# Windowed attention and SoLU feed-forward: the first tile's product block by block, w_in's differences on VectorE, scores moved on TensorE

## The chip, the cores and the metric

The kernel runs on one core of one Trainium2 chip. The metric is the time of one execution on the device in microseconds (us), as the median of several runs. A core has TensorE (PE in the rows; PEld are its weight loads), VectorE (DVE), ScalarE (ACT), GpSimd (POOL) and SyncE (SP), which here issues every DMA. Each engine takes its instructions in order; engines wait for each other by semaphores.

## The reference

Attention over a window of 64 keys, 8 batches of 576 positions with 8 heads of 64, and behind it a feed-forward layer with softmax gating and a normalization:

```python
scores = scale * np.matmul(q, k.transpose(0, 1, 3, 2))
scores = np.where((rel >= 0) & (rel < 64), scores, -1000000000.0)
attn = np.exp(scores - np.max(scores, axis=-1, keepdims=True))
attn = attn / (np.sum(attn, axis=-1, keepdims=True) + 1e-09)
x = np.matmul(attn, v)                  # heads joined: 4608 x 512
h = x @ w_in                            # 512 x 1024
e = np.exp(h - np.max(h, axis=-1, keepdims=True))
solu = h * (e / (np.sum(e, axis=-1, keepdims=True) + 1e-09))
ln = (solu - mu) / np.sqrt(var + 1e-06) * g_ln      # mean and variance of a row
return ln @ w_out                       # 1024 x 512
```

## The kernel before

The 4608 rows are 36 tiles of 128. A tile passes these steps, which are functions in the code (t is the tile):

- `scores(t)` (L376): 32 small matmuls of q and k into pS, of which there is one buffer. For a tile in `MASKED` (tiles 1 to 5) two more matmuls (L384) put the mask into pS first.
- `softmax(t)` (L407): for a tile in `MASKED`, VectorE takes the maximum out of pS by two reductions (L421), and eight exponentials on ScalarE (L437) read pS. For later tiles one VectorE instruction (L428) moves pS with scale and mask to sS, another (L433) takes the maximum, and the exponentials read sS. The scaling by the inverse sum, eight instructions (L452), is VectorE's for tiles below `SCALES` = 3 and GpSimd's from there.
- `transposes(t)` (L495), for tiles below 8: eight transposes on TensorE, copied in two halves to PT (L511); the second half by VectorE from tile `EARLY` = 3, else by ScalarE. From tile 8 the probabilities are turned by DMA instead (`soft_planes`, `soft_turn`: pd<-raw, raw<-pd).
- `values(t)` (L523): 32 matmuls with v into pX; ScalarE copies pX to xH (L538, L540), VectorE makes the rest xL (L541, from tile 3).
- `moe_in(t, h)` (L552): half h of the product with w_in into pH (one buffer). Tiles below `PLAIN_IN` = 3 use the plain float32 weights W32 in four matmuls a half (L556; two instructions each in the trace); later tiles use three passes with weights and x in two parts (L567).
- `moe_norm(t)` (L572): maximum (L582), exponential (L584), product and sum (L587), square (L593) and some small steps, then the scaling of e on GpSimd (L604).
- `moe_transpose(t)`, or by DMA `planes` and `turn`; then `moe_out(t)` (L679) with w_out: L685 for tile 0, L695 from tile 1, and the output copy ot (L702).

The weights come as int64 words of doubles, in eight blocks: 0 to 3 are w_in, 4 to 7 w_out. `weight_block` (L287) converts each by one ScalarE and four VectorE steps (L308 to L315); w_out is also multiplied by g on GpSimd (L319). `split(i)` (L330) makes the two parts of a block: ScalarE rounds each half to WH (L333), and the difference WL of half 0 is made by VectorE and that of half 1 by GpSimd (L336). The tiles WL lie in the same ring of nine buffers as W32: WL of block i + 1 overwrites W32 of block i, and so waits for all that reads that block, the differences of block i among it.

The order is made by a planner when the program is built. TensorE keeps the order in which the code lists the steps (but for the transposes, values and scores of tiles 0 and 1). The other engines' steps, SyncE's DMAs among them, get due times from it, counted back through the listed costs, and are placed by a list schedule. Where the schedule has TensorE idle, matmuls on the identity are put in (pO_filler, L784), until the first output product.

The loop from L736 lists, for each t below `BEHIND` = 3: both halves of `moe_in(t)`, `moe_norm(t)`, `planes(t)`, `transposes(t + 1)`, scores and softmax of tile t + 3, `values(t + 1)`. For t = 0 scores and softmax of tile 2 stand between the halves. From t = 3: `moe_in(t, 0)`, `transposes(t + 1)`, `moe_in(t, 1)`, `moe_norm(t)`, `planes(t)`, `moe_transpose(t - 3)`, `values(t + 1)`, the scores of the tiles in `ahead(t)`, `moe_out(t - 3)`. `ahead` gives tile 6 at t = 3, tiles 7 and 8 at t = 4, and t + 4 from there on. `split` of w_in is listed at t = 3, that of w_out at t = 4.

Of the kernel before, what the change touches and what calls it, by code (L numbers as in the profile page):

```python
# [24 lines left out]
NEG = -1.0e9  # L25

AHEAD = 3
FURTHER = 4

HASTE = 1  # L30
# [1 line left out]
LOOSE = 2  # L32
BEHIND = 3

EARLY = 3

JOINS = 8

PLANES = 4

HEADS = 1
MASKED = range(1, 6)
SCALES = 3

PLAIN_IN = 3
PLAIN_OUT = 1

BY_DMA = (1, 2)
# [137 lines left out]
def tile_window_attention_solu_moe(  # L186
# [17 lines left out]
    nc = tc.nc  # L204
# [125 lines left out]
    def split(i):  # L330

        for x in range(2):
            plan.op("ACT", 600, lambda x=x: nc.scalar.copy(WH(i, x), W32(i)[:, x]),  # L333
                    [("w", i), ("w", i, x), ("w", NC + 1 if i < NC else NW - 1)], [("H", i, x)])
            engine, eng, cost = (("DVE", nc.vector, 690), ("POOL", nc.gpsimd, 1450))[x]
            plan.op(engine, cost, lambda x=x, eng=eng: eng.tensor_sub(  # L336
                WL(i)[:, x], W32(i)[:, x], WH(i, x).bitcast(F32)),
                [("w", i), ("w", i, x), ("H", i, x)], [("w", NW + i, x)])
# [213 lines left out]
    def moe_in(t, h):  # L552
        hs = slice(h * 512, (h + 1) * 512)
        if t < PLAIN_IN:
            for c in range(NC):
                plan.op("PE", 930, lambda c=c: nc.tensor.matmul(  # L556
                    PH(t)[:, hs], XH(t)[:, c], W32(c)[:, h],
                    start=(c == 0), stop=(c == NC - 1)),
                    [("xH", t), ("w", c), ("w", c, h)], [("pH", t)])
            return  # L560
        passes = [(c, *k) for c in range(NC) for k in (
            (XH, WH, "xH", "H", 0), (XH, WL, "xH", "w", NW), (XL, WH, "xL", "H", 0))]
        if t == PLAIN_IN:

            passes.sort(key=lambda k: k[4] == "w")
        for n, (c, x, w, xk, wk, o) in enumerate(passes):
            plan.op("PE", 233, lambda n=n, c=c, x=x, w=w: nc.tensor.matmul(  # L567
                PH(t)[:, hs], x(t)[:, c], WH(c, h) if w is WH else WL(c)[:, h],
                start=(n == 0), stop=(n == len(passes) - 1)),
                [(xk, t), (wk, o + c, h)], [("pH", t)])  # L570
# [108 lines left out]
    def moe_out(t):  # L679
# [22 lines left out]
        plan.op("ACT", 580, lambda: nc.scalar.copy(ot(), PO()), [("pO", t)], [("ot", t)])  # L702
        plan.dma(P * DM * 4, lambda: nc.sync.dma_start(out[t * P:(t + 1) * P, :], ot()), [("ot", t)], [])

    def on(f, t, *args):
        if 0 <= t < NTILE:
            f(t, *args)
# [28 lines left out]
    for t in range(NTILE + BEHIND):  # L736
# [4 lines left out]
            for i in range(NC):  # L741
                split(i)
        on(moe_in, t, 0)
        if t == 0:
            scores(2)
            softmax(2)
        if t < BEHIND:
            on(moe_in, t, 1)
            on(moe_norm, t)
            on(planes, t)  # L750
            on(transposes, t + 1)
            on(scores, t + AHEAD)
            on(softmax, t + AHEAD)
            on(soft_planes, t + AHEAD)
            on(soft_turn, t + AHEAD)
            on(join, t + 1)
            on(values, t + 1)
        else:
            on(transposes, t + 1)
            on(moe_in, t, 1)  # L760
            on(moe_norm, t)
            on(planes, t)
            if t - BEHIND < NTILE - BY_DMA[1]:
                on(moe_transpose, t - BEHIND)
            on(join, t + 1)
            on(values, t + 1)
            for a in ahead(t):
                on(scores, a)
                on(softmax, a)
                on(soft_planes, a)  # L770
                on(soft_turn, a)
            if t - BEHIND == PLAIN_OUT:
                for i in range(NC, NC + NF // 2):
                    split(i)
            if t - BEHIND + 1 >= NTILE - BY_DMA[1]:
                on(moe_transpose, t - BEHIND + 1)
            on(moe_out, t - BEHIND)

    plan.first = [("qk", 0), ("raw", 0), ("v", 0), ("qk", 1), ("raw", 1), ("raw", 2), ("raw", 3), ("v", 1), ("qk", 2)]
    def filler(n):  # L780
# [53 lines left out]
```

## Time and profile before

| | |
|---|---|
| median of 3 runs | 548.37 us (546.87 to 548.4) |
| profiled execution | 549.3 us; its span, first to last instruction, 547.5 us |
| TensorE (PE) busy | 530.9 us, 97% of the span |
| VectorE (DVE) | 367.4 us, 67% |
| ScalarE (ACT) | 330.3 us, 60% |
| GpSimd (POOL) | 292.9 us, 53% |
| chain that ended last | PE 84%, DVE 7%, POOL 3%, DMA 2% |

The page gives busy time per engine over the whole span, which is an average over unlike stages: the start, in which the weights are converted and the first tiles pass, the steady part, and the end. The rows further down are from views of the same execution that look at one stage, one engine or one line. TensorE's busy time includes the filling matmuls, and matmuls overlap, so a matmul's cost in a row of them is the distance from start to start. A releaser behind an idle time is the instruction that the waiting one waited for last. The granted clock is TensorE's, 1.00 for 2.4 GHz and 0.50 for 1.2 GHz.

### The profile page before, as it was taken

To read this page: it belongs to the slowest core of one execution; us is meant where nothing else is said; L and a number is where in the kernel's file an instruction comes from. 1 tells how busy PE (TensorE), PEld (TensorE's weight loads), DVE (VectorE), ACT (ScalarE), POOL (GpSimd) and SP (SyncE) were. 2 spreads that over 40 slices of the span, in tenths; PEclk is the share of its full clock that TensorE was granted. 3 is DMA by queue.
4 is the path that set the end of the run, shared out by engine and by line. 5 is a ranking of instruction groups with operands and counts; after the bars stand their busy time and mean duration, and the time that the engine had idled before them with its cause. 6 is when DMAs were issued, how large, how long until landed. Compare 5 with 4: busy or idle time off the path is not lost.

```text
span 547.5 us, 11649 instructions
## 1 busy us (share of the span) xinstructions
PE 530.9 (97%) x4250; PEld 416.9 (76%) x4250; DVE 367.4 (67%) x725; ACT 330.3 (60%) x955; POOL 292.9 (53%) x490
## 2 busy tenths in 40 slices
PE   8799799899999999999999999999999999999996
PEld 7565486688877877778778777777877777777885
DVE  4999758766666666666666666666666677655530
ACT  4468475576666666666666666656666666663330
POOL 5214988664555555555555555555555555671110
PEclk9999989899999999999999999999999999999999
DMA  8963115647999999999999999999999994787211
GB/s 355 403 262 116 48 59 168 209 146 208 236 255 233 242 246 237 257 234 242 241 256 231 246 261 217 243 262 222 262 243 237 246 233 155 189 235 174 59 38 38
DMA packets 153081, 115.58 MB, mean 211 GB/s; under 512 B 129856, under 2 KB 129856, under 8 KB 152512
## 3 DMA queue, kind: packets, MB, share of 16 engines
q1 hardware_dynamic: 153024, 114.84, 81.0%
q8 instruction: 33, 0.54, 0.4%
q14 instruction: 24, 0.20, 0.1%
HBM read 41.42 MB, written 41.42 MB: 151 GB/s over the span
## 4 chain that ended last, share of the span: by engine, by line
PE 84%; DVE 7%; POOL 3%; issue 2%; DMA 2%; ACT 1%; SPq 0%; POOLq 0%; ACTq 0%
PE pO L695 35%; PE pH L567 33%; PE pX L530 6%; PE pS L400 5%; DMA raw<-pd 2%; DVE w L313 1%; PE pO L685 1%; DVE w L315 1%; PE pH L556 1%; POOL e L604 1%; DVE w L309 1%; PE t L506 1%; DVE sS L452 1%; POOL w L336 1%; POOL sS L452 1%
## 5 line engine op out<-in xcount | busy, mean ns | idle before, releaser
L452 POOL TENSOR_SCALAR sS<-sS,rec 128x128 f32<-128x128 f32 x264 | 117.4, 467 | 147.1 <-DVE rec L449 144.7
L695 PE MATMUL pO<-w_outH,yH 128*128 128x512 f32 x280 | 115.3, 412 | 0.7 <-ACT ot L702 0.7
L695 PE MATMUL pO<-w,yH 128*128 128x512 f32 x280 | 111.6, 399 | 0.0
L695 PE MATMUL pO<-w_outH,yL 128*128 128x512 f32 x280 | 110.6, 395 | 0.0
L567 PE MATMUL pH<-w_inH,xH 128*128 128x512 f32 x264 | 106.5, 403 | 0.0
L567 PE MATMUL pH<-w,xH 128*128 128x512 f32 x264 | 104.2, 398 | 0.0
L567 PE MATMUL pH<-w_inH,xL 128*128 128x512 f32 x264 | 104.1, 394 | 0.0
L437 ACT ACTIVATE sS<-sS,nmx 128x128 f32<-128x128 f32 x248 | 96.2, 390 | 9.6 <-DVE nmx L433 4.7
L702 ACT COPY ot<-pO 128x512 f32<-128x512 f32 x36 | 21.1, 587 | 97.8 <-PE pO L695 77.4
L584 ACT ACTIVATE e<-pH,mst 128x1024 f32<-128x1024 f32 x36 | 40.2, 1118 | 59.1 <-DVE mst L582 58.8
L582 DVE TENSOR_REDUCE mst<-pH 128x1 f32<-128x1024 f32 x36 | 44.1, 1224 | 42.0 <-PE pH L567 42.0
L604 POOL TENSOR_SCALAR e<-e,mst 128x512 f32<-128x512 f32 x72 | 60.1, 843 | 16.8 <-DVE mst L601 14.9
L596 DVE SCALAR_TENSOR_TENSOR mst<-mst 128x1 f32<-128x1 f32 x36 | 27.8, 772 | 60.1 <-ACT pl L593 60.1
L695 PEld LDWEIGHTS pO<-w_outH,yH 128*128 128x128 f32 x280 | 52.9, 189 | 18.0 <-issue 4.8
L695 PEld LDWEIGHTS pO<-w_outH,yL 128*128 128x128 f32 x280 | 53.0, 189 | 13.2
L695 PEld LDWEIGHTS pO<-w,yH 128*128 128x128 f32 x280 | 52.9, 189 | 10.9
L567 PEld LDWEIGHTS pH<-w_inH,xH 128*128 128x128 f32 x264 | 49.9, 189 | 13.2 <-ACT sS L437 0.2
L567 PEld LDWEIGHTS pH<-w_inH,xL 128*128 128x128 f32 x264 | 50.1, 190 | 12.4
L567 PEld LDWEIGHTS pH<-w,xH 128*128 128x128 f32 x264 | 49.6, 188 | 11.4 <-issue 0.2
L472 POOL COPY raw<-sS 128x1024 uint16<-128x1024 uint16 x56 | 56.7, 1043 | 0.0
L437 ACT ACTIVATION_READ_ACCUMULATOR sS<-sS,nmx 128x1 f32 x248 | 46.6, 188 | 0.0
L663 DVE TENSOR_TENSOR yL<-yT,yH 128x512 fp32r<-128x512 f32 x66 | 44.5, 708 | 2.6 <-ACT yH L661 2.6
(95 smaller groups left out, 867.0 us busy)
## 6 DMA issues: line engine op xcount, KB each, us to landing
qk<-qk SPq DMA_DIRECT2D x36, 640.0 KB, 5.9
yd<-pl SPq DMA_DIRECT2D x33, 512.0 KB, 6.6
pd<-raw SPq DMA_DIRECT2D x28, 512.0 KB, 3.7
v<-vS SPq DMA_DIRECT2D x36, 256.0 KB, 3.4
y<-ot SPq DMA_DIRECT2D x36, 256.0 KB, 3.1
raw<-w_in SPq DMA_DIRECT2D x4, 1024.0 KB, 10.6
raw<-w_out SPq DMA_DIRECT2D x4, 1024.0 KB, 8.6
yT<-yd SPq DMA_TRANSPOSE x33, 4.8
```

The source lines that it names most:

```text
L400: nc.tensor.matmul(PS(t)[half * WIN:(half + 1) * WIN, r, p], q[rs, p, half * WIN:(half + 1) * WIN], keys, start=t not in MASKED, stop=t no ...
L437: plan.op("ACT", 580, lambda h=h: nc.scalar.activation(SS(t)[:, h], PS(t)[:, h // NPAIR, h % NPAIR] if t in MASKED else SS(t)[:, h], AF.Ex ...
L452: plan.op(engine, cost, lambda h=h: v.tensor_scalar(SS(t)[:, h], SS(t)[:, h], rec()[:, h:h + 1], 0.0, ALU.mult, ALU.add), [("rec", t)], [( ...
L472: plan.op(engine, cost, lambda x=x, copy=copy: copy(PP(t)[:, :, 4 * x:4 * x + 4].rearrange("p k h n -> p k (h n)"), SS(t)[:, 4 * x:4 * x + ...
L530: nc.tensor.matmul(PX(t)[r * D:(r + 1) * D, p, ks], (V if half else VX)(t)[:, h * D:(h + 1) * D], PT(t)[:, r * NPAIR + p, ks], start=True, ...
L567: plan.op("PE", 233, lambda n=n, c=c, x=x, w=w: nc.tensor.matmul(PH(t)[:, hs], x(t)[:, c], WH(c, h) if w is WH else WL(c)[:, h], start=(n ...
L582: plan.op("DVE", 1230, lambda: nc.vector.tensor_reduce(nmax(), PH(t), axis=AX.X, op=ALU.max, negate=True), [("pH", t)], [key(0)])
L584: plan.op("ACT", 1320, lambda: nc.scalar.activation(E(t), PH(t), AF.Exp, bias=nmax(), scale=1.0, accum_out=se()), [("pH", t), key(0)], H2 ...
L596: plan.op("DVE", 130, lambda: nc.vector.scalar_tensor_tensor(kk(), se(), se(), ss(), ALU.mult, ALU.mult), [key(1), key(3)], [key(5)])
L604: plan.op("POOL", 770, lambda h=h, hs=hs: nc.gpsimd.tensor_scalar(E(t)[:, hs], E(t)[:, hs], nmean(), kk(), ALU.add, ALU.mult), [key(4), ke ...
L663: plan.op("DVE", 690, lambda hs=hs: nc.vector.tensor_sub(YL(t)[:, hs], YT(t)[:, hs], YH(t)[:, hs].bitcast(F32)), [("yT", t), ("yH", t, h)] ...
L695: plan.op("PE", 233, lambda f=f, i=i, x=x, k=k, y=y, w=w: nc.tensor.matmul(PO(), y(t)[:, f], w(i, x), start=(f == k == 0), stop=(f == NF - ...
```

## The change

1. Tile 0's product with w_in is listed block by block, both halves of a block one behind the other (`WIDE`), and no longer half by half. Scores and softmax of tile 2 stand behind the whole product (`PLACES`).
2. Tiles 2 and 3 are no longer in `MASKED`; the scaling of tile 2 is GpSimd's (`SCALES` = 2); both halves of tile 3's PT are ScalarE's (`EARLY` = 4).
3. All eight differences of w_in are VectorE's; those of w_out stay as they were.
4. Where `ahead(t)` has two tiles (t = 4), the second one's scores and softmax stand behind `moe_out(t - 3)`.
5. From t = `SWAP` = 5 the scores of tile t + 4 stand ahead of `values(t + 1)`.

The planner's listed cost of a plain matmul goes from 930 to 870.

```diff
+SWAP = 5
+
+PLACES = {2: (0, 0), 3: (0, 2), 4: (1, 2), 5: (2, 2)}
...
-EARLY = 3
+EARLY = 4
...
-MASKED = range(1, 6)
-SCALES = 3
+MASKED = (1, 4, 5)
+SCALES = 2
 
 PLAIN_IN = 3
+WIDE = 1
...
-            engine, eng, cost = (("DVE", nc.vector, 690), ("POOL", nc.gpsimd, 1450))[x]
+            engine, eng, cost = (("DVE", nc.vector, 690), ("POOL", nc.gpsimd, 1450))[x * (i >= NC)]
...
         if t < PLAIN_IN:
+            both = t < WIDE
+            if both and h:
+                return
             for c in range(NC):
-                plan.op("PE", 930, lambda c=c: nc.tensor.matmul(
-                    PH(t)[:, hs], XH(t)[:, c], W32(c)[:, h],
-                    start=(c == 0), stop=(c == NC - 1)),
-                    [("xH", t), ("w", c), ("w", c, h)], [("pH", t)])
+                for x in range(2) if both else (h,):
+                    plan.op("PE", 870, lambda c=c, x=x: nc.tensor.matmul(
+                        PH(t)[:, x * 512:(x + 1) * 512], XH(t)[:, c], W32(c)[:, x],
+                        start=(c == 0), stop=(c == NC - 1)),
+                        [("xH", t), ("w", c), ("w", c, x)], [("pH", t)])
             return
...
+    def attend(t):
+        scores(t)
+        softmax(t)
+        soft_planes(t)
+        soft_turn(t)
+
+    def first_tiles(t, place):
+        for a, at in PLACES.items():
+            if at == (t, place):
+                attend(a)
...
-        if t == 0:
-            scores(2)
-            softmax(2)
         if t < BEHIND:
+            first_tiles(t, 0)
             on(moe_in, t, 1)
             on(moe_norm, t)
             on(planes, t)
+            first_tiles(t, 1)
             on(transposes, t + 1)
-            on(scores, t + AHEAD)
-            on(softmax, t + AHEAD)
-            on(soft_planes, t + AHEAD)
-            on(soft_turn, t + AHEAD)
+            first_tiles(t, 2)
             on(join, t + 1)
             on(values, t + 1)
+            first_tiles(t, 3)
         else:
...
-            on(join, t + 1)
-            on(values, t + 1)
-            for a in ahead(t):
-                on(scores, a)
-                on(softmax, a)
-                on(soft_planes, a)
-                on(soft_turn, a)
+            if t < SWAP:
+                on(join, t + 1)
+                on(values, t + 1)
+            for a in ahead(t)[:1]:
+                on(attend, a)
+            if t >= SWAP:
+                on(join, t + 1)
+                on(values, t + 1)
             if t - BEHIND == PLAIN_OUT:
                 for i in range(NC, NC + NF // 2):
                     split(i)
...
             on(moe_out, t - BEHIND)
+            for a in ahead(t)[1:]:
+                on(attend, a)
```

## Rows read from the trace of the kernel before

**Rows 1.** Stretches: busy us (instructions) of each engine, granted clock, DMA share, GB/s

```profile
30.00:60.00 30.00, 29.43 (x251) 17.91 (x244) 28.51 (x57) 23.85 (x73) 13.41 (x19) 1.00 0.39 138
...
66.50:73.00 6.50, 6.49 (x46) 5.91 (x47) 5.89 (x15) 5.10 (x17) 6.22 (x11) 0.52 0.13 40
...
141.50:155.05 13.55, 13.55 (x113) 10.81 (x112) 9.35 (x18) 8.77 (x26) 7.71 (x14) 1.00 1.00 232
```

**Rows 2.** TensorE's waits, whole span: us in total, times, longest

```profile
PE pX L530 <- DMA raw<-pd: 0.7, 1, 0.7
```

**Rows 3.** TensorE's time line, product 0: start, us, instruction, idle before, releaser

```profile
25.74 1.13 PE L556 MATMUL pH<-w,xH 128*128 128x512 f32 x2 [2.10 <-DVE w L315]
...
28.13 1.12 PE L556 MATMUL pH<-w,xH 128*128 128x512 f32 x2 [0.16 <-DVE w L315]
...
30.66 3.70 PE L556 MATMUL pH<-w,xH 128*128 128x512 f32 x8
```

**Rows 4.** TensorE's time line from tile 3's scores to product 3

```profile
38.58 0.59 PE L384 MATMUL pS<-maskNoneB,identB 128*128 128x512 bf16 x2
...
40.13 7.13 PE L556 MATMUL pH<-w,xH 128*128 128x512 f32 x16
...
47.10 1.04 PE L506 MATMUL t<-ident,sS 128*128 128x128 f32 x8
...
50.62 1.60 PE L784 MATMUL pO_filler<-ident 128*128 128x128 f32 x12
...
52.79 7.10 PE L556 MATMUL pH<-w,xH 128*128 128x512 f32 x16 [0.57 <-DVE mst L587]
...
59.73 1.04 PE L506 MATMUL t<-ident,sS 128*128 128x128 f32 x8
...
66.51 0.37 PE L530 MATMUL pX<-PT,vx 128*64 128x64 f32 x1 [4.01 <-DVE PT L511]
...
70.56 0.77 PE L567 MATMUL pH<-w_inH,xH 128*128 128x512 f32 x1
```

**Rows 5.** GpSimd's and VectorE's time lines at the differences of w_in

```profile
62.73 1.26 POOL L336 TENSOR_TENSOR w<-w,w_inH 128x512 fp32r<-128x512 f32 x1
...
64.03 0.69 DVE L336 TENSOR_TENSOR w<-w,w_inH 128x512 fp32r<-128x512 f32 x1 [2.54 <-POOL w L336]
```

**Rows 6.** Instruction groups: VectorE 28-82, GpSimd 28-100 (busy, mean ns); then L336 (min/median/max)

```profile
L421 DVE TENSOR_REDUCE nmx<-pS 128x4 f32<-128x512 f32 x8 | 5.2, 676 | 0.9 <-PE pS L400 0.9
...
L428 DVE SCALAR_TENSOR_TENSOR sS<-pS,maskNone 128x1024 f32<-128x1024 f32 x1 | 1.2, 1225 | 0.8 <-PE pS L400 0.8
...
L452 DVE TENSOR_SCALAR sS<-sS,rec 128x128 f32<-128x128 f32 x16 | 3.7, 296 | 0.1
...
L336 DVE TENSOR_TENSOR w<-w,w_inH 128x512 fp32r<-128x512 f32 x4 | 2.7, 686 | 2.5 <-POOL w L336 2.5
...
L452 POOL TENSOR_SCALAR sS<-sS,rec 128x128 f32<-128x128 f32 x32 | 12.8, 424 | 2.8 <-DVE mst L596 2.4 <-DVE rec L449 0.4
...
L336 POOL TENSOR_TENSOR w<-w,w_inH x4: 1258/1272/2236, 53.6 to 69.0; 128x512 fp32r<-128x512 f32 x4
```

**Rows 7.** VectorE's last difference of w_out, then TensorE's time line at scores 8

```profile
93.18 2.31 DVE L336 TENSOR_TENSOR w<-w,w_outH 128x512 fp32r<-128x512 f32 x1
...
98.79 1.10 PE L400 MATMUL pS<-qk 64*64 64x128 f32 x32 [1.92 <-DVE sS L428]
...
99.83 0.59 PE L695 MATMUL pO<-w_outH,yH 128*128 128x512 f32 x1
...
103.58 0.39 PE L695 MATMUL pO<-w_outH,yH 128*128 128x512 f32 x1
```

**Rows 8.** A steady tile: VectorE's xL, then TensorE's next product

```profile
200.57 0.69 DVE L541 TENSOR_TENSOR xL<-pX,xH 128x512 fp32r<-128x512 f32 x1
...
203.60 0.40 PE L567 MATMUL pH<-w_inH,xH 128*128 128x512 f32 x1
...
203.84 0.40 PE L567 MATMUL pH<-w,xH 128*128 128x512 f32 x1
```

More of the change, by code (lines that the diff above doesn't have):

```diff
@@ L750, in tile_window_attention_solu_moe @@
             on(planes, t)
+            first_tiles(t, 1)
             on(transposes, t + 1)
-            on(scores, t + AHEAD)
-            on(softmax, t + AHEAD)
-            on(soft_planes, t + AHEAD)
-            on(soft_turn, t + AHEAD)
+            first_tiles(t, 2)
             on(join, t + 1)
             on(values, t + 1)
+            first_tiles(t, 3)
         else:
+            first_tiles(t, 0)
             on(transposes, t + 1)
```

## The prediction

> **What bounds the kernel now.** I read the table of stretches first, then TensorE's waits, then the time lines of the first 110 us. From about 107 us on the kernel is TensorE: in a tile of the steady part it is busy 13.55 of 13.55 us, and VectorE 9.35 [rows 1]. In all the steady part one wait of it shows, 0.7 us for transposed probabilities [rows 2]. So nothing can be won there but the 0.7 us, and the stage that decides is the beginning. There TensorE is filled up with matmuls on the identity and waits; VectorE is busy 28.51 of 30 us from 30 to 60 us, and from 66.5 to 73 us the granted clock is 0.52, so half the time at the lower of the two levels (1.2 against 2.4 GHz) [rows 1]. I call the products with w_in of tile t "product t".
>
> **Part 1: product 0 block by block.** Now its first half waits for the blocks of w_in as VectorE converts them: block 2 at 25.74 after a wait of 2.10 us, block 3 at 28.13. The second half stands whole behind, 30.66 to 34.36, eight instructions in 3.70 us [rows 3]. After, both halves of blocks 0 to 2 run in the waits, and behind block 3 (still 28.13) stand four instructions, 3.70 / 2 = 1.85 us: product 0 ends at 30.0 instead of 34.4. On TensorE's own queue six of the eight late instructions go, 2.8 us; the normalization of tile 0 starts 4.4 us sooner. The cover is the conversion on VectorE, whose order before block 3 I take as kept; a slip by one step of a conversion is the other end, 1.2 us by the nearest row of that size (L428) [rows 6].
>
> **Part 2: tiles 2 and 3 without mask matmuls.** TensorE loses two instructions per tile, 0.5 to 0.6 us. More important, pS (one buffer) comes free after one VectorE instruction instead of after eight exponentials: the mask matmuls of tile 3 stood until 38.58, so product 1 began at 40.13 [rows 4]. VectorE pays: 1.23 and about as much again (a second pass over the same 1024 columns) instead of 2 x 0.68 per tile, 2 x 1.1 = 2.2 us. The scaling of tile 2 leaves VectorE (8 x 0.30 = 2.4 us at most) and costs GpSimd 8 x 0.42 = 3.4 us [rows 6]. GpSimd has little to do at that time, and this is hidden as long as it ends before product 1 does; if not, it delays the transposes of tile 2 by at most those 3.4 us.
>
> **Part 3: differences of w_in on VectorE, second half of tile 3's PT on ScalarE.** GpSimd loses four instructions of 1.26 to 2.24 us, 6 us together; VectorE gains 4 x 0.69 = 2.7 us and loses one copy of a difference's size, 0.7 [rows 6]. What this undoes is a chain of two in-order queues. The difference of block 1's second half stands on GpSimd behind the scaling of e and runs at 62.73. The ring of w makes VectorE's difference of block 2 overwrite the block which that one reads, so VectorE waits 2.54 us, until 64.03. Behind it in VectorE's queue stand the maximum of tile 2 and the PT copy of tile 3 [rows 5], and values 3 waits 4.01 us for that copy, until 66.51 [rows 4]. After, all eight differences are in one queue and need only TensorE's last read of the block above. Net load added to VectorE by parts 2 and 3: 2.2 - 2.4 + 2.7 - 0.7 = +1.8 us.
>
> GpSimd's difference took between 1.26 and 2.24 us for the same shape, VectorE's 0.69 [rows 6]. The Trainium skill (SBUF — State Buffer, Who interferes with whom) says that a VectorE instruction with two SBUF inputs and a GpSimd instruction that reads SBUF shut each other out for their whole length. By it the four moved differences would take 4 x 0.69 = 2.7 us of GpSimd's time back, and the time would come out up to 2.7 us later (539.2) if GpSimd were still last in the gap. The one long row agrees with that rule, the other three do not show it; after the move GpSimd is no longer waited for there, and the sum goes without it.
>
> **The gaps between products, and the sum of the beginning.** Between product 1 (ends 47.1) and product 2 (52.79) lie 5.7 us: maximum, exponential and sum that free pH, beside transposes, scores and values. That gap had no GpSimd in it, so I take it for all gaps of the changed kernel. Product 0 ends at 30.0; product 1 runs from 35.7 for 6.97 us (40.13 to 47.10) to 42.7; product 2 from 48.4 for 6.94 us to 55.3. Before product 3 the difference xL comes on top and VectorE has the differences of w_in to make between: 7 us instead of the present 10.8 (59.73 to 70.56), hence 62.3 against 70.56, 8.3 us [rows 4]. The bounds of a gap: from below TensorE's own work in it, 3.5 us (47.10 to the filling matmuls at 50.62: transposes, scores, values); from above 10.8 [rows 4]. With the wait of 4 us I expect the lower clock to go as well: until 73 us some five matmuls of product 3 run at it [rows 1], at 0.42 us from start to start instead of 0.24 (the two spacings of [rows 7, 8]), 0.9 us. Beginning: 9.2 us.
>
> **Part 4: scores 8 behind the second tile's output product.** Tiles 7 and 8 now have their scores one behind the other, and with one pS the second waits 1.92 us for VectorE; the clock then drops, and nine matmuls take 3.75 us (99.83 to 103.58, 0.42 each) instead of 9 x 0.24 = 2.15 [rows 7]. Moving scores 8 gives back 1.9 + 1.6 = 3.5 us. What is late next there is the output product itself, which now starts 3 us sooner; its last operand, a difference of w_out, ends at 95.5, 1.4 us before scores 7 does (98.79 - 1.92 = 96.87) [rows 7], so the move alone leaves it free. The load of the next q and k moves with the scores; it waits for its buffer then as now.
>
> **Part 5: scores ahead of values from tile 5.** The same instructions in another order. Values come later by the length of the scores, 1.04 us (98.79 to 99.83) [rows 7], so the 0.7 us wait for the transposed probabilities goes. What is queued behind values: xH, then xL on VectorE, which is done at 201.2 where the next product starts at 203.60 [rows 8], 2.4 us of cover for the 1.04; if it is gone, the excess is paid in each of some 30 tiles. On SyncE the load of v, which waits for values, now stands behind that of q and k, which waits for scores; the later of the two goes at the same moment, so the transposes behind them do not move. A change from the product to scores directly is in no row; I bound it by plus and minus 0.1 us a tile, under half of the 0.24 us between two matmuls (3 us in all), and take zero. Gain 0.7.
>
> **The sum.** 9.2 + 3.5 + 0.7 = 13.4 us. Against it stands VectorE's 1.8 us in a stretch where it is already 95% busy; I take 1.5 of it as paid on the path (ends: 0, and 5 if VectorE becomes what is last in every gap). Gain 11.9 us on the profiled execution of 549.3 us (span 547.5), so 537.4; the median of the runs is 0.9 below that execution, hence **536.5 us**.
>
> **The rivals.**
> - VectorE takes GpSimd's place (chance 0.24). It converts w_out, makes eight differences and serves three softmaxes; if steps on the chain stand behind conversions of 1.2 us, the gap before product 3 stays near 10.8, with the lower clock: 3.8 + 0.9 + about 0.5 elsewhere back: 541.7. For it: 28.51 of 30 us [rows 1]. Against it: the 2.54 us that VectorE stood waiting for GpSimd [rows 5] are room for nearly all of the 2.7 us that it takes over.
> - The stall moves (0.10): the output product of tile 1 waits in place of scores 8, for its yL or the last difference of w_out, because everything before it came 9 us sooner and GpSimd still makes half of those: 3.5 back, 540. Against it the 1.4 us of slack.
> - More than I forecast (0.08): the first two gaps shrink to TensorE's own 3.5 us and 1.1 (1.1 less each), the third to 5.7 (1.3 less), and the 1.5 is not paid: 5.0 less, 531.5.
> - Slower (0.06): the transposed probabilities. In the steady part the DMA engines are busy the whole time (share 1.00 [rows 1]); the larger load (q and k against v) now goes ahead, and the transposes behind may land later. It decides where they land more than 1.04 us later than now plus what slack there is; then values wait in each of the 28 tiles from tile 8 on, at the price seen once, 0.7 us [rows 2]: 19.6 us, 556. Against it: one of 28 waits now, and values come later.
> - No gain on balance (0.04): the order of the early VectorE work changes with the products and block 3 comes late by as much as is won: 547.
>
> **The numbers.** Forecast 0.48, 536.5, by itself 533 to 540. The range from 531.5 (the best case) to 545 (the first two rivals together: 536.5 + 5.2 + 3.5) leaves out the slower case, the one without gain and a little more. A measurement of this kernel tells about 0.3% from no change, 1.6 us: faster 0.88, within 0.05, slower 0.07.
>
> **What would show it.** Product 0 ending near 30 us with two products for each block; no wait of VectorE for GpSimd's differences; product 3 starting at 60 to 64 us, at the full clock; no wait of scores 8 and none put in its place before the output product of tile 1; a steady tile of 13.55 us as now. Wrong would be the prediction if TensorE waited over 3 us at any point between 30 and 100 us, or if a steady tile took more than 13.6 us.

## The result, and the profile after

The changed kernel takes 540.46 us (median of six runs, 540.08 to 542.04) where the kernel before, run beside it, takes 547.68 (six runs). The ratio is 0.9868, 95% interval 0.9838 to 0.9898: 7.2 us faster. Two of the six executions (541.90 and 542.04 us) show a mean granted clock of 0.995, the other four 0.999 or 1.000. The forecast was 536.5 us in a range from 531.5 to 545: the time lies in the range, and the gain is 7.2 us where 11.2 had been forecast against that median. The profiled execution of the changed kernel took 540.08 us, its span is 538.2 against 547.5.

The changed file has other line numbers: the scaling by the inverse sum is L456 now (L452 before), product with w_in L564 and L575 (L556, L567), scores L404 (L400), first output products L693 and L703 (L685, L695), differences L340 (L336), maximum of a product L590 (L582), the two steps of the inverse sum L450 and L453 (L446, L449).

First the page of the changed kernel (busy us, share of the span, instructions) and TensorE's waits (us in total, times, longest):

```profile
PE 527.3 (98%) x4236; PEld 411.6 (76%) x4236; DVE 372.7 (69%) x716; ACT 331.0 (62%) x956; POOL 303.3 (56%) x494
...
PE t L510 <- POOL sS L456: 1.9, 3, 1.0
...
PE pH L564 <- DVE w L319: 1.4, 1, 1.4
...
PE t L665 <- POOL e L612: 0.4, 1, 0.4
```

The waits for the PT copy (4.0 us), for scores 8 (1.9) and for the transposed probabilities [rows 2, 4, 7] are gone. A new one stands first: transposes of probabilities wait for GpSimd's scalings. The stretches (columns as in [rows 1]) show the beginning and a steady part of 100 us:

```profile
36.00:50.00 14.00, 12.70 (x101) 7.04 (x101) 12.65 (x23) 9.68 (x34) 7.43 (x12) 1.00 0.21 69
50.00:62.50 12.50, 12.48 (x106) 7.51 (x105) 12.48 (x20) 10.09 (x30) 12.28 (x13) 1.00 0.31 100
62.50:76.00 13.50, 12.40 (x119) 9.58 (x118) 11.94 (x28) 8.55 (x27) 11.57 (x18) 1.00 0.12 40
...
200.00:300.00 100.00, 100.00 (x862) 79.84 (x861) 69.19 (x134) 64.67 (x189) 57.39 (x93) 1.00 0.90 244
```

TensorE is at the full clock (1.00) in all four, and the steady part has no gap. GpSimd, which had 13.41 us of work between 30 and 60 us [rows 1], is busy 12.28 of 12.5 us from 50 us on. TensorE's time line (start, us, instruction, idle before) has the marks that answer to [rows 3, 4]:

```profile
28.07 1.98 PE L564 MATMUL pH<-w,xH 128*128 128x512 f32 x4
29.89 1.04 PE L510 MATMUL t<-ident,sS 128*128 128x128 f32 x8
...
35.80 7.11 PE L564 MATMUL pH<-w,xH 128*128 128x512 f32 x16
...
46.53 0.33 PE L510 MATMUL t<-ident,sS 128*128 128x128 f32 x1 [0.98 <-POOL sS L456]
...
50.15 7.13 PE L564 MATMUL pH<-w,xH 128*128 128x512 f32 x16
57.12 1.43 PE L510 MATMUL t<-ident,sS 128*128 128x128 f32 x8
...
62.62 0.47 PE L575 MATMUL pH<-w_inH,xH 128*128 128x512 f32 x1
...
65.99 1.01 PE L510 MATMUL t<-ident,sS 128*128 128x128 f32 x4
...
68.44 1.02 PE L510 MATMUL t<-ident,sS 128*128 128x128 f32 x3 [0.66 <-POOL sS L456]
69.22 0.48 PE L575 MATMUL pH<-w_inH,xH 128*128 128x512 f32 x1
...
75.77 7.13 PE L693 MATMUL pO<-w,yH 128*128 128x512 f32 x16
```

Product 0 ends at 29.9, product 1 starts at 35.80, product 2 at 50.15, product 3 at 62.62, and the first output product at 75.77, where it was 81.20 before. So 7.9 us are won at the start of product 3, but only 5.4 at the first output product: 2.5 are lost again between the two, although the lower clock, which cost time just there before, is gone. In that stretch the transposes of tile 4 (65.99 and 68.44) stand between the two halves of product 3 and wait for GpSimd's scaling. Last, scores 8:

```profile
91.45 0.50 PE L703 MATMUL pO<-w_outH,yH 128*128 128x512 f32 x1
...
97.36 1.10 PE L404 MATMUL pS<-qk 64*64 64x128 f32 x32
98.39 0.50 PE L575 MATMUL pH<-w_inH,xH 128*128 128x512 f32 x1
```

From the end of scores 7 to the next product it is 98.39 - 91.45 = 6.9 us, against 107.08 - 96.87 = 10.2 before [rows 7, with the product that follows there]: 3.3 us.

### The profile page after: what moved, and what is told of

Same layout as the page of the kernel before. It is cut to its first block, busy times and chain, and to the rows that moved or that the text cites. A ratio compares the mean times of both kernels' runs of the same rounds, so it can differ in the third digit from the quotient of the medians.

```text
span 538.2 us, 11654 instructions
## 1 busy us (share of the span) xinstructions
PE 527.3 (98%) x4236; PEld 411.6 (76%) x4236; DVE 372.7 (69%) x716; ACT 331.0 (62%) x956; POOL 303.3 (56%) x494
## 4 chain that ended last, share of the span: by engine, by line
PE 86%; DVE 7%; POOL 3%; issue 2%; ACT 1%; POOLq 0%; ACTq 0%
PE pO L703 37%; PE pH L575 33%; PE pX L534 6%; PE pS L404 6%; POOL sS L456 2%; DVE w L317 1%; PE pO L693 1%; DVE w L313 1%; DVE w L319 1%; DVE w L340 1%; PE pH L564 1%; PE t L510 1%; DVE w L315 1%; POOL e L612 0%; DVE nmx L425 0%
## 5 line engine op out<-in xcount | busy, mean ns | idle before, releaser
L456 POOL TENSOR_SCALAR sS<-sS,rec 128x128 f32<-128x128 f32 x272 | 126.7, 484 | 139.5 <-DVE rec L453 102.6
L703 PE MATMUL pO<-w_outH,yH 128*128 128x512 f32 x280 | 114.7, 410 | 0.7 <-ACT ot L710 0.7
L703 PE MATMUL pO<-w,yH 128*128 128x512 f32 x280 | 111.0, 396 | 0.0
L703 PE MATMUL pO<-w_outH,yL 128*128 128x512 f32 x280 | 110.1, 393 | 0.0
L441 ACT ACTIVATE sS<-sS,nmx 128x128 f32<-128x128 f32 x264 | 102.4, 391 | 10.6 <-DVE nmx L437 6.2
L575 PE MATMUL pH<-w_inH,xH 128*128 128x512 f32 x264 | 105.9, 401 | 0.0
L575 PE MATMUL pH<-w,xH 128*128 128x512 f32 x264 | 104.2, 398 | 0.0
L575 PE MATMUL pH<-w_inH,xL 128*128 128x512 f32 x264 | 103.7, 393 | 0.0
L612 POOL TENSOR_SCALAR e<-e,mst 128x512 f32<-128x512 f32 x72 | 66.7, 933 | 15.6 <-DVE mst L609 7.7
L703 PEld LDWEIGHTS pO<-w_outH,yH 128*128 128x128 f32 x280 | 52.5, 187 | 15.1 <-ACT ot L710 1.1
L703 PEld LDWEIGHTS pO<-w_outH,yL 128*128 128x128 f32 x280 | 52.6, 188 | 13.3 <-DVE yL L671 0.3
L703 PEld LDWEIGHTS pO<-w,yH 128*128 128x128 f32 x280 | 52.6, 188 | 10.8
L590 DVE TENSOR_REDUCE mst<-pH 128x1 f32<-128x1024 f32 x36 | 44.0, 1221 | 23.6 <-PE pH L575 22.8
L575 PEld LDWEIGHTS pH<-w_inH,xH 128*128 128x128 f32 x264 | 49.5, 188 | 13.1 <-ACT sS L441 0.2
L575 PEld LDWEIGHTS pH<-w_inH,xL 128*128 128x128 f32 x264 | 49.6, 188 | 12.5
L575 PEld LDWEIGHTS pH<-w,xH 128*128 128x128 f32 x264 | 49.6, 188 | 11.4 <-issue 0.2
L635 DVE COPY pl<-e 128x1024 uint16<-128x1024 uint16 x60 | 42.9, 715 | 21.3 <-POOL e L612 20.3
L710 ACT COPY ot<-pO 128x512 f32<-128x512 f32 x36 | 21.0, 585 | 53.9 <-issue 38.2
L671 DVE TENSOR_TENSOR yL<-yT,yH 128x512 fp32r<-128x512 f32 x66 | 50.9, 800 | 3.2 <-ACT yH L669 2.9
L601 ACT ACTIVATE pl<-e,mst 128x1024 bf16<-128x1024 f32 x36 | 41.4, 1149 | 18.2 <-issue 14.8
## 6 DMA issues: line engine op xcount, KB each, us to landing
raw<-w_in SPq DMA_DIRECT2D x4, 1024.0 KB, 10.8
```

Of the source, the lines that this page charges most:

```text
L441: plan.op("ACT", 580, lambda h=h: nc.scalar.activation(SS(t)[:, h], PS(t)[:, h // NPAIR, h % NPAIR] if t in MASKED else SS(t)[:, h], AF.Ex ...
L456: plan.op(engine, cost, lambda h=h: v.tensor_scalar(SS(t)[:, h], SS(t)[:, h], rec()[:, h:h + 1], 0.0, ALU.mult, ALU.add), [("rec", t)], [( ...
L590: plan.op("DVE", 1230, lambda: nc.vector.tensor_reduce(nmax(), PH(t), axis=AX.X, op=ALU.max, negate=True), [("pH", t)], [key(0)])
L601: plan.op("ACT", 1330, lambda: nc.scalar.activation(PL(t)[:, 0].bitcast(BF16), E(t), AF.Square, bias=nmean(), scale=1.0, accum_out=ss()), ...
L612: plan.op("POOL", 770, lambda h=h, hs=hs: nc.gpsimd.tensor_scalar(E(t)[:, hs], E(t)[:, hs], nmean(), kk(), ALU.add, ALU.mult), [key(4), ke ...
L635: plan.op(engine, cost, lambda h=h, hs=hs, eng=eng: eng.tensor_copy(PL(t)[:, :, hs], E(t)[:, hs].bitcast(U16).rearrange("p (n k) -> p k n" ...
```

## The experiments

Two theories stood against each other for what the forecast had put too low, the price on the path of the work that changed its engine. **Load**: VectorE's queue has 1.8 us more, and chain steps stand behind it. **Lock**: GpSimd's scalings are slow because VectorE's instructions shut it out of SBUF, and TensorE waits for them. Each run below is told by its span (538.2 is the changed kernel's), its ratio to the kernel before with the interval, and the starts of product 2, product 3 and the first output product (50.15, 62.62 and 75.77 in the changed kernel). The first product starts between 19.9 and 20.7 us in all of them; where that matters it is said.

Spans of one kernel differ by up to 2 us between executions (538.2 to 540.1 us for the changed kernel), so a smaller difference of spans shows nothing by itself, nor do ratios whose intervals overlap. The starts repeat better where the clock does not fall: in a4_scores8_old and b1_no_swap, whose edits act only after 90 us, all three agree with the changed kernel's within 0.15 us.

### Each part undone

**Part 1.** Half by half again:

```diff
-WIDE = 1
+WIDE = 0
```

> The changed kernel with tile 0's product half by half again, scores 2 between the halves. By the forecast's term, product 0 ends near 34.3 us instead of 29.9 and product 1 starts 2.8 to 4.4 us later; the kernel is 2.8 to 4.4 us slower than the changed one (span 541.0 to 542.6 against 538.2). By the rival, that GpSimd's scalings of tiles 2 to 4 set the pace of the beginning, part of it is hidden: under 1.5 us, since GpSimd's scaling of tile 2 (41.0 to 46.5 us) would still be what the transposes of tile 2 wait for.

Span 540.0, ratio 0.9876 (0.9853 to 0.9898). Product 0 ends at 33.7 and product 1 starts at 38.89, 3.1 us later, as the forecast's term has it. Products 2 and 3 are 4.4 and 4.3 us later. Some 1.3 us of that is the lower clock, which this execution shows from 49 to 52 us, behind two waits of 0.45 us for GpSimd's scalings (a time line, then a stretch):

```profile
50.29 1.99 PE L404 MATMUL pS<-qk 64*64 64x128 f32 x32
...
49.00:52.00 3.00, 2.97 (x35) 1.95 (x35) 0.00 (x0) 2.20 (x4) 3.00 (x7) 0.50 0.00 0
```

Yet the first output product comes at 77.81, only 2.0 us later: half of what part 1 wins is taken up between product 3 and the output product. What does it is the end of GpSimd's scaling of tile 4, 68.8 us here and 69.1 in the changed kernel. Here TensorE comes to tile 4's transposes at 69.9 and does not wait; in the changed kernel it is ready for them at 65.6 and waits. By the ratio alone (0.9876 against 0.9868) the part's worth can't be told from nothing.

**Part 2, the masks.** Tiles 2 and 3 masked again:

```diff
-MASKED = (1, 4, 5)
+MASKED = range(1, 6)
```

> The changed kernel with the mask matmuls of tiles 2 and 3 again. By the forecast's term scores 3 wait for eight exponentials and product 1 starts 2 to 4 us later than 35.8; VectorE saves 2.2 us. If the stretch between product 3 and the first output product is what sets the end, part of that is absorbed there, as it was with product 0 half by half: span 538.2 to 540.5; otherwise 540 to 542.

Span 538.6, ratio 0.9866 (0.9830 to 0.9903). Product 1 starts at 39.17, 3.4 us later; product 3 at 64.73, 2.1 later; the first output product at 75.25, 0.5 us sooner than with the change. All of what this part wins at product 1 is absorbed before the output product, at the same place: the scaling of tile 4 ends at 66.7 us here, and its transposes at 68.5 do not wait. With the other parts in place, this one is worth nothing that the runs can tell.

**Part 3, the differences.** GpSimd's again:

```diff
-(...)[x * (i >= NC)]
+(...)[x]
```

> The changed kernel with the second halves' differences of w_in on GpSimd again. By the forecast's term the chain of two queues comes back: VectorE waits for GpSimd's differences, values 3 waits 3 to 4 us, the clock drops, span 542 to 545 against 538.2. By the rival (moving them only shifts load between two engines that shut each other out) the span stays within 1.5 us of 538.2.

Span 542.5, ratio 0.9931 (0.9906 to 0.9955): 4.3 us of span, of which 0.6 is a first product that starts later (20.7 us); 3.4 us by the ratio. TensorE's waits, then a line of VectorE's time line:

```profile
PE t L510 <- POOL sS L456: 2.3, 3, 1.0
...
PE pH L575 <- DVE mst L595: 1.5, 1, 1.5
PE pO L703 <- ACT yH L669: 1.4, 1, 1.4
...
PE pO L703 <- DVE yL L671: 0.7, 1, 0.7
...
60.41 1.17 DVE L340 TENSOR_TENSOR w<-w,w_inH 128x512 fp32r<-128x512 f32 x1 [1.27 <-POOL w L340]
```

The amount is the forecast's, the form only in part. VectorE waits for a difference of GpSimd's again, 1.27 us, and product 3 then 1.5 us for the sum that VectorE makes behind it; so the chain of two queues is there. The wait of 4 us at values 3 and the lower clock do not come back: the copy that values 3 waited for stays ScalarE's in this run. Product 3 starts at 65.29, the first output product at 77.81, and the second one waits 1.4 us for yH and 0.7 for yL, because GpSimd scales e of tile 1 later (from 79.4 us instead of 75.7). The moved differences undo that chain and relieve GpSimd behind it as well. The other half of part 3, the copy on ScalarE (`EARLY`), was not undone by itself, nor was the planner's new cost.

**Part 4, scores 8.** Right behind scores 7 again:

```diff
-            for a in ahead(t)[:1]:
+            for a in ahead(t):
                 on(attend, a)
...
-            for a in ahead(t)[1:]:
-                on(attend, a)
```

> The changed kernel with scores 8 right behind scores 7 again. By the forecast's term 1.9 us of waiting and 1.6 us of lower clock come back: span 541 to 542 against 538.2. If the lower clock came from the longer wait at values 3, which the changed kernel no longer has, only the wait returns: 1.9, span 540.1.

Span 542.0, ratio 0.9916 (0.9887 to 0.9946): 3.8 us. The wait and the lower clock both return, in this time line of TensorE:

```profile
93.63 1.76 PE L404 MATMUL pS<-qk 64*64 64x128 f32 x32 [1.96 <-DVE sS L432]
95.32 0.79 PE L703 MATMUL pO<-w_outH,yH 128*128 128x512 f32 x1
```

The scores take 1.76 us to record in place of 1.10, the output product starts at 95.32 instead of 91.45. The granted clock is 0.91 from 90 to 110 us, against 1.00 in the changed kernel. It fell here without the 4 us wait at values 3, directly behind this wait of 1.96 us.

The same edit alone, on the kernel before:

```diff
-            for a in ahead(t):
+            for a in ahead(t)[:1]:
...
             on(moe_out, t - BEHIND)
+            for a in ahead(t)[1:]:
+                on(scores, a)
+                on(softmax, a)
+                on(soft_planes, a)
+                on(soft_turn, a)
```

> The kernel before with one edit: scores and softmax of tile 8 behind the output product of tile 1. By the forecast's term the wait of 1.9 us and the lower clock behind it go: 3.5 us, span 544.0 against 547.5. If the stall moves to the output product instead (yL or the last difference of w_out late), 0 to 1.5 us.

Span 545.0 against 547.5, ratio 0.9969 (0.9946 to 0.9991). From the end of scores 7 to the next product it takes 104.67 - 97.83 = 6.8 us against 10.2: 3.4 us, as forecast. But product 1 starts at 41.39 where it was 40.13, and scores 7 end 1.0 us later. The early steps stand in the same order in both traces, on TensorE and on VectorE; what differs is the clock. Behind the same wait of 2.10 us, the stretch from 26 to 29 us is at the lower level here and at the full one in the profiled execution of the kernel before (a row of this run's time line, then that stretch here and in the kernel before):

```profile
25.75 2.08 PE L556 MATMUL pH<-w,xH 128*128 128x512 f32 x2 [2.10 <-DVE w L315]
...
26.00:29.00 3.00, 3.00 (x9) 1.97 (x10) 2.96 (x8) 1.16 (x1) 0.00 (x0) 0.50 1.04 407
...
26.00:29.00 3.00, 2.84 (x14) 1.70 (x14) 2.96 (x8) 1.16 (x1) 0.00 (x0) 1.00 1.04 408
```

So this microsecond is nothing that the edit is seen to cause.

**Part 5, the swap.**

```diff
-SWAP = 5
+SWAP = 99
```

> The changed kernel with values ahead of scores in all tiles. By the forecast's term the steady tile stays 13.54 us, and at most 0.7 us of waiting for transposed probabilities comes back (span 538.2 to 538.9). If the order of the two matters in every tile (a change from product to scores that is cheaper or dearer), the span moves by up to 3 us.

Span 538.4, ratio 0.9870 (0.9820 to 0.9921). TensorE has no wait for transposed probabilities in it, with values ahead of scores as before. So the 0.7 us that I booked for the swap is not the swap's: such a wait comes and goes. With the swap, b2_masked had one of 0.8 us in one tile, the changed kernel none; without it, the kernel before had one of 0.7 and b4_scores8_alone one of 0.5. A steady tile is 13.54 us either way.

### Where GpSimd's time goes

**Tile 2's scaling on VectorE again** (part 2's other half):

```diff
-SCALES = 2
+SCALES = 3
```

> The changed kernel with tile 2's scaling on VectorE again (2 us of VectorE's queue, before product 1 ends). If VectorE's added load is what ate the missing 2 to 4 us, the kernel gets slower by 0.5 to 2 us. If GpSimd's scaling, 5.5 us in place of 3.4, is what the transposes of tile 2 waited for, that wait (1.2 us, and 0.7 us of filling matmuls) goes, product 2 starts at 48.3 to 49 instead of 50.15, and the span falls by 0.5 to 2 us.

Span 539.9, ratio 0.9884 (0.9857 to 0.9911). Product 2 starts at 48.73 (with the first product 0.5 us later than in the changed kernel), 1.9 us sooner on that account: GpSimd's scaling of tile 2, 5.5 us, was what its transposes waited for. Then product 3 waits 2.8 us for the rounded w_in, and the clock is 0.87 from 62.5 to 76 us (a wait and a stretch of TensorE's, then a line of GpSimd's time line and two of VectorE's):

```profile
PE pH L575 <- ACT w_inH L337: 2.8, 1, 2.8
...
62.50:76.00 13.50, 12.34 (x113) 10.19 (x113) 13.50 (x23) 9.85 (x30) 10.82 (x16) 0.87 0.01 2
...
49.22 6.33 POOL L456 TENSOR_SCALAR sS<-sS,rec 128x128 f32<-128x128 f32 x8 [0.34 <-DVE rec L453]
...
56.90 0.16 DVE L609 TENSOR_TENSOR mst<-mst 128x1 f32<-128x1 f32 x1 [2.29 <-POOL mst L608]
...
59.15 1.21 DVE L590 TENSOR_REDUCE mst<-pH 128x1 f32<-128x1024 f32 x1
```

ScalarE's queue had stood 2.9 us for the maximum of product 2, which VectorE began at 59.15, although the product ended at 55.7. It looks like load, but for 2.29 us of that time VectorE stood idle itself: it waited for a small step of tile 0's normalization (L608), which GpSimd made only behind its scaling of tile 3, 6.33 us long. Only the rest, two conversion steps ahead of the maximum, is VectorE's queue. The first output product comes at 75.93, and the second one waits 1.3 us for yH.

**The scaling of tiles 2 to 4 on ScalarE:**

```diff
+        if t in (2, 3, 4):
+            for h in range(H):
+                plan.op("ACT", 300, lambda h=h: nc.scalar.activation(
+                    SS(t)[:, h], SS(t)[:, h], AF.Copy, scale=rec()[:, h:h + 1]),
+                    [("rec", t)], [("sS", t, h)])
+            return
```

> The changed kernel with the scaling of tiles 2, 3 and 4 on ScalarE, eight copies with a scale of about 0.39 us each, 3.1 us a tile. If GpSimd's scalings are what is late between product 1 and the first output product, TensorE's waits for them (1.9 us and the filling matmuls beside them) go and the span falls by 1 to 3 us. If ScalarE's queue becomes late in their place (it copies PT, xH and the rounded w_in there), the span stays within 1 us or grows.

Span 545.6, ratio 1.0005 (0.9983 to 1.0027): the whole gain is lost. Product 2 starts at 48.32 and product 3 at 60.64, 2 us sooner each; but 24 copies more stand in ScalarE's queue, product 3 waits there for the rounded w_in, e of tile 0 comes 1.4 us late, and the second output product waits 1.3 us for yH and 3.0 for yL, with the lower clock behind it (0.91 from 90 to 110 us). ScalarE is busy 60% of the whole span, but 12.08 of 14 us from 36 to 50.

**VectorE's conversions of w_out without what shuts GpSimd out.** The four steps of a block give way to three maxima, of about the same length and place; the conversion of w_out is left out:

```diff
+        if g is not None:
+            for _ in range(3):
+                plan.op("DVE", 1230, lambda: nc.vector.tensor_reduce(
+                    tf()[:, 0, 0:1], tf().rearrange("p a n -> p (a n)"), axis=AX.X, op=ALU.max), [W], [W])
...
+            return
```

> The changed kernel, but the four VectorE steps that convert a block of w_out (two of 0.6 us with one SBUF input, two of 1.15 us with two SBUF inputs) are replaced by three maxima over the same 1024 columns (1.13 us each, one input): about the same time in VectorE's queue, 3.4 against 3.5 us a block. The conversion of w_out is left out, so what the second product computes is not the reference's. If GpSimd is slow because VectorE's conversions shut it out, GpSimd's scalings of tiles 2 and 3 (5.5 and 8.2 us for eight) fall to 2.8 to 3.5 us, TensorE's waits for them go, and the first output product starts 1 to 3 us sooner (span 535 to 537 against 538.2). If it is the load in VectorE's queue, the first output product starts within 0.5 us of 75.8 and the span stays.

Span 535.0 (the longest of this kernel's four executions; the others took 533.5 to 533.9), ratio 0.9788 (0.9745 to 0.9831). GpSimd's scalings of tiles 2, 3 and 4 (eight instructions each), in the changed kernel, then here, where the scaling is L464:

```profile
41.01 5.47 POOL L456 TENSOR_SCALAR sS<-sS,rec 128x128 f32<-128x128 f32 x8 [6.68 <-DVE rec L453]
49.96 8.21 POOL L456 TENSOR_SCALAR sS<-sS,rec 128x128 f32<-128x128 f32 x8
64.34 4.73 POOL L456 TENSOR_SCALAR sS<-sS,rec 128x128 f32<-128x128 f32 x8 [1.56 <-DVE rec L453]
```

```profile
40.91 2.80 POOL L464 TENSOR_SCALAR sS<-sS,rec 128x128 f32<-128x128 f32 x8 [6.47 <-ACT sS L449]
48.15 2.81 POOL L464 TENSOR_SCALAR sS<-sS,rec 128x128 f32<-128x128 f32 x8
56.55 4.25 POOL L464 TENSOR_SCALAR sS<-sS,rec 128x128 f32<-128x128 f32 x8
```

5.47 and 8.21 us become 2.80 and 2.81, with VectorE busy 13.86 of 14 us from 36 to 50 (12.65 in the changed kernel): that the kind of VectorE's instructions slows GpSimd's is shown, and it isn't the load. Product 2 starts at 48.71, 1.4 us sooner; product 3 at 60.90, 1.7 sooner; the first output product at 71.24, 4.5 us sooner. But the last 2.8 us of those arise between product 3 and the output product, and there another thing has changed: tile 4's scaling starts at 56.55 instead of 64.34.

**Only the one-input steps taken out.** Two of the four steps, those with one SBUF input, give way to one maximum; the two-input steps stay:

```diff
-        plan.op("DVE", 700, lambda: nc.vector.tensor_scalar(
-            tf(), tf(), EXP_LO, EXP_HI, ALU.max, ALU.min), [W], [W])
-        plan.op("DVE", 700, lambda: nc.vector.tensor_scalar(
-            t(), t(), 0x07FFFFFF, 3, ALU.bitwise_and, ALU.logical_shift_left), [W], [W])
+        if g is not None:
+            plan.op("DVE", 1230, lambda: nc.vector.tensor_reduce(
+                tf()[:, 0, 0:1], tf().rearrange("p a n -> p (a n)"), axis=AX.X, op=ALU.max), [W], [W])
+        else:
...
```

> The changed kernel, but of the four VectorE steps that convert a block of w_out only the two with one SBUF input (0.6 us each) are replaced, by one maximum over the same columns; the two with two SBUF inputs (1.15 us each) stay. That part of the conversion is left out, so the second product is not the reference's. If the two-input steps shut GpSimd out, GpSimd's scalings of tiles 2 and 3 stay well over the 2.8 us that they took without any of the steps (5.5 and 8.2 with all), by about the two-input steps' share of the time, two thirds: 4.5 and 6 us, and the first output product starts between 73 and 75.8 us. If the one-input steps do it, the scalings fall to about 3 us and the first output product starts near 71.2 us.

Span 534.7, ratio 0.9829 (0.9781 to 0.9877). The scalings of tiles 2 and 3 take 4.73 and 5.15 us, between the two others: the two-input steps slow GpSimd, and the one-input steps add to it (the scaling is L460 here, the inverse sum L454 and L457).

```profile
40.62 4.73 POOL L460 TENSOR_SCALAR sS<-sS,rec 128x128 f32<-128x128 f32 x8 [6.48 <-ACT sS L445]
...
48.96 5.15 POOL L460 TENSOR_SCALAR sS<-sS,rec 128x128 f32<-128x128 f32 x8
...
57.12 4.26 POOL L460 TENSOR_SCALAR sS<-sS,rec 128x128 f32<-128x128 f32 x8
```

Product 2 starts at 49.89 and product 3 at 62.16 (with the first product 0.2 us sooner than in the changed kernel), so nothing of note is won there; yet the first output product starts at 72.50, 3.1 us sooner on that account, and sooner than the 73 us that I had put as its lower end. What did that is tile 4's scaling: it starts at 57.12 instead of 64.34, and is hardly shorter. One reason stands in VectorE's time line, the two steps of tile 4's inverse sum, in the changed kernel and here:

```profile
59.31 0.16 DVE L450 TENSOR_SCALAR rec<-sm 128x8 f32<-128x8 f32 x1
...
63.96 0.19 DVE L453 RECIPROCAL rec<-rec 128x8 f32<-128x8 f32 x1
```

```profile
53.87 0.27 DVE L454 TENSOR_SCALAR rec<-sm 128x8 f32<-128x8 f32 x1
...
54.17 0.20 DVE L457 RECIPROCAL rec<-rec 128x8 f32<-128x8 f32 x1
```

The exponentials of tile 4 end at 53.9 in the changed kernel. The sum's inverse, two instructions of 0.2 us, is placed at 59.3 and 64.0, behind differences of w_in, the product's sum and xL. Only then can GpSimd scale; its 4.73 us end at 69.1, and TensorE's transposes of tile 4, for which it is ready at 65.6 us, end 2.9 us late. In c1_no_lock and c2_two_input the planner happened to put the inverse at 54.5 and 54, and no transposes of tile 4 waited there.

The inverse is not the whole of it. In the changed kernel GpSimd stood idle for it only 1.56 us (its line at 64.34 above); until 62.8 us it had other work, at the end two copies of vx, which in c1_no_lock and c2_two_input stand behind the scaling. And the scaling itself took 4.73 us, where the eight instructions took 2.80 in c1_no_lock for tile 2: that is 1.9 us more, also on the path. Each of the two would win part of the 2.9 us; no run changes only one of them.

**Tile 3's scaling on VectorE, tile 2's left on GpSimd:**

```diff
-("POOL", nc.gpsimd, 400) if t >= SCALES else
+("POOL", nc.gpsimd, 400) if t >= SCALES and t != 3 else
```

> The changed kernel with tile 3's scaling on VectorE (1.6 to 2 us there in place of 8.2 on GpSimd); tile 2's stays on GpSimd. If GpSimd shut out is what costs the beginning 4.5 us, this frees it at 50 to 58 us: tile 4's scaling and tile 0's e come sooner and the first output product starts 0.5 to 2 us sooner, span 536 to 538. If VectorE's queue then becomes late at product 3, as with tile 2's scaling on it, the span grows by 1 to 2 us.

Span 539.5, ratio 0.9900 (0.9862 to 0.9938). The longest of GpSimd's scalings, 8.2 us, is off it, and nothing comes sooner: first output product 76.23 (first product 0.4 us later). Tile 4's scaling still starts at 64.8, and TensorE's wait is the same (1.9 us in all, three times), since VectorE's inverse comes as late:

```profile
64.41 0.20 DVE L453 RECIPROCAL rec<-rec 128x8 f32<-128x8 f32 x1
...
64.80 4.73 POOL L456 TENSOR_SCALAR sS<-sS,rec 128x128 f32<-128x128 f32 x8 [2.12 <-DVE rec L453]
```

GpSimd, relieved of 8.2 us, stands idle for 2.12 us in front of tile 4's scaling. So tile 3's slow scaling costs nothing on the path of the changed kernel, with the inverse where it is; VectorE's 2.0 us for it are in that balance. In a3_scale2_dve, where a step of tile 0's normalization stands behind it, VectorE waits for it.

**Tiles 2 and 3 both on VectorE:**

```diff
-SCALES = 2
+SCALES = 4
```

> The changed kernel with the scaling of tiles 2 and 3 on VectorE. By the queue's load 4 us more in VectorE's queue from 39 to 56 us: product 3 starts 1 to 3 us later than 62.6 with the lower clock, span 540 to 542. By the lock alone GpSimd is free of 13.7 us of scaling, the first output product starts 1 to 3 us sooner, span 535.5 to 537.5.

Span 539.1, ratio 0.9886 (0.9849 to 0.9924), between the two forecasts. Product 2 starts at 48.64, 2 us sooner on the same account, product 3 at 62.05 after 1.1 us of waiting for rounded weights, and within it TensorE waits 1.8 us for differences from VectorE; first output product 76.56. VectorE is busy all of the time from 50 to 76 us, so what the freed GpSimd gives, VectorE's queue takes back. None of the variants that compute the whole result is faster than the changed kernel by more than the noise (b2_masked has 0.9866 and b1_no_swap 0.9870, against 0.9868).

## Why the prediction was right in its range, and where its sum was off

- **Part 1**: right as a step. Product 0 ends at 29.9 (30.0 forecast), product 1 starts at 35.80 (35.7), with the gap of 5.7 us taken from product 1 to 2 of the kernel before. Undone, it costs 3.1 us at product 1, but 2.0 at the first output product, and by the ratio nothing that can be told.
- **Part 2**: the sentence that failed first. I wrote that GpSimd has little to do at that time, and that the scaling of tile 2 is hidden as long as it ends before product 1 does. It took 5.47 us instead of the 3.4 in the sum, ended at 46.5, and product 1 at 42.7. It began only at 41.0, when VectorE had the inverse sum, so that even 3.4 us would have ended past product 1. I had taken the gap of 5.7 us because it "had no GpSimd in it"; this part put GpSimd into it, and it measured 7.4. I had named the price if it did not stay hidden, up to 3.4 us; product 2 came at 50.15 instead of 48.4. Run a3_scale2_dve gives 1.9 us for it, c1_no_lock 1.4.
- **The rule set aside** (the Trainium skill, SBUF — State Buffer, Who interferes with whom): I weighed the lock only for the four differences and left the sum without it, since GpSimd would no longer be last. The rule was right where I did not apply it, on GpSimd's own scalings beside VectorE's conversions. By c1_no_lock it is worth 1.4 us on the path, for tile 2; for tile 3 it lengthens the scaling most (8.21 us) and costs nothing in the changed kernel (d2_scale3_dve); for tile 4 it can be up to 1.9 us of the loss before the first output product, which no run here isolates.
- **Part 3**: right in size (4.3 us of span when undone). The chain that I described is part of it (VectorE waits 1.27 us, product 3 then 1.5); the rest is GpSimd's queue, which is later behind that without the part.
- **The gap before product 3**: 5.5 us measured, 7 taken, 10.8 before. Product 3 started at 62.62 (62.3 forecast). That it came so near is luck: product 2 was 1.75 us late, and this gap 1.5 us shorter than I took it. The clock stayed full, as forecast. I read the granted clock of 0.52 from 66.5 to 73 us as half the time at the lower level; 0.50 is that level, so it was nearly all the time. The 0.9 us taken for it does not rest on the half.
- **What was not in the sum at all**: the way from product 3 to the first output product. I carried it over from the kernel before (10.6 us, less 0.9 for the clock); it took 13.15. Of the 3.4 us between, 2.9 are tile 4's transposes, which wait for GpSimd's scaling. It starts late, for 1.56 us because of the inverse sum in VectorE's queue, and it is slow beside VectorE. The first is the first rival's mechanism, chain steps behind VectorE's other work, at another place than I gave it; the second is the rule set aside. With the 1.5 us given back on VectorE's account, the beginning was to bring 7.7 and brought 5.4. How the 2.9 us divide stays open: a run that moves the two instructions of the inverse and nothing else was not made.
- **Part 4**: 3.3 us measured, 3.5 forecast; 3.8 when undone, 3.4 in place when made alone. The output product did not take over the stall.
- **Part 5**: zero, not 0.7. The one wait that I booked comes and goes with either order.
- **From execution to median**: the sum gave 537.4 for the profiled execution, which took 540.08; of that miss of 2.7 us the beginning is 2.3 (7.7 less 5.4) and part 4 0.2. The 0.7 us of part 5 does not appear in it, because the kernel before had such a wait in its profiled execution and the changed one did not. I then took off 0.9, as the profiled execution of the kernel before stood above its median. The changed one's stands 0.4 below its own. These 1.3 us are the rest of the 4.0 by which 536.5 missed 540.46.

## What to carry to other kernels

When an edit makes one stage early, look at the next stage for steps that were early enough only because the stage ahead was late: here one scaling on GpSimd, started late behind a 0.2 us instruction on VectorE and slowed by VectorE's other work, took back 2.9 us. When an engine is late, ask whether it was busy or itself waiting: in a3_scale2_dve VectorE looked overloaded and had stood idle for GpSimd. Cost an instruction that is moved to another engine by what that engine does beside its neighbour at that very time, not by its mean over the kernel: the same scaling took 2.8 and 8.2 us. And a part that wins time at its own place can be worth nothing at the end (the masks), so undo each part in the finished kernel before crediting it. Before putting a shift of a microsecond down to an edit, compare the granted clock of that stretch in both traces.

## What the runs showed of the hardware

- Eight scalings of 128x128 on GpSimd take 2.80 us beside maxima on VectorE, 4.73 to 5.15 beside conversion steps with two SBUF inputs, 5.47 to 8.21 when steps with one input stand among them (tiles 2 and 3 of c1_no_lock, c2_two_input and the changed kernel). The Trainium skill (SBUF — State Buffer, Who interferes with whom) names VectorE instructions with two SBUF inputs, and `tensor_scalar` in a mode that uses both ports, as ones that contend with GpSimd, and `tensor_reduce` on this chip as one that never does; these runs agree with it, though none shows the mode in which the one-input steps ran.
- The length of one wait on TensorE does not tell whether the clock falls behind it. It fell behind waits of 1.96 us (a4_scores8_old) and 2.8 us (a3_scale2_dve), and behind two of 0.45 us (a1_half_order); in the changed kernel it fell behind none of up to 1.4 us. Behind the same wait of 2.10 us it stayed full in the profiled execution of the kernel before [rows 3] and fell in that of b4_scores8_alone, which is the same up to there; the fall cost 1.3 us at product 1.
- One wait of 0.5 to 0.8 us for a DMA in a steady tile came and went between the traces, without regard to the order of scores and values (there in the kernel before, b4_scores8_alone and b2_masked, not in the changed kernel and b1_no_swap).
